# Windowed attention, router and experts: queries and keys turned by DVE in squares of 32, scores of four heads in four row groups

## The chip, the cores and the metric

The program runs on one core of one Trainium2 chip. The metric is the time of one execution on the device in microseconds. The kernel before takes 577.99 us, the median of 3 runs (576.69 to 580.51).

A core has a matrix engine PE (with its weight loads, PEld), a vector engine DVE, a scalar engine ACT, a general engine POOL, and SP, which here only issues transfers. Each runs its own instructions in order; semaphores tie them together.

## The reference

```
scores = (q @ k.T) / sqrt(64)          # q, k, v: batch 4, heads 8, tokens 768, width 64
keep   = key < n_global  or  0 <= query - key < n_local      # 8 and 96 in the given inputs
a      = softmax(where(keep, scores - slope[h] * distance, -1e9))
x      = (a @ v), heads side by side                          # 3072 tokens x 512
logits = normalized(x) @ normalized(expert_emb).T / tau       # 8 experts
e      = argmax(logits);  gate = softmax(logits)[e]
out    = gate * (relu(x @ w1[e]) @ w2[e])                     # w1[e]: 512 x 1024
```

All numbers are float32.

## The kernel before, in words

A group is four heads of one batch, a pair is two of these heads. There are eight groups. Keys come in eight blocks of 96; because the window is at most 97 keys long, a block of keys is scored against its own 96 queries and the next 96. Thirty more key rows per block hold the first tokens of the sequence, the global keys. One block with its 126 key rows is a unit, two units make a step, four steps a group: 32 steps in all, in the loop over `steps` in `window_attention`. The last batch's two groups are interleaved by halves.

`load_tokens` (L367) brings q and k of a pair with token on partition, 128 tokens at a time, in runs of 64 numbers; `load_v` brings v (L373) and its global rows, repeated for each block (L374). SP issues them, two groups ahead. `turn` transposes three tiles of 128x128 with PE (L399) into a PSUM bank, two heads side by side, and ACT copies them to `kT` (L401, L406 for the global rows) and `qT` (L404). `score` (L418) multiplies the 64 rows of each head in one of two row groups of PE: four matmuls a unit, two banks. `grow` takes exp on ACT (L422) and `weigh` multiplies with a table of decay and mask on DVE (L429). `attend` does the step before: output (L444), sums of weights (L452), and after every second step copies out of PSUM: `xd` by ACT (L457) and DVE (L458), `den` by DVE (L463, L465).

When both groups of a batch have finished half of their queries, that half goes through phases, one a step (`half_turns`): PE turns x back to tokens (L516), DVE divides by the sums (L521) and SP stores it, ACT squares it (L526), and the router `choose` works on DVE (L196 to L242), PE, ACT and POOL; POOL then writes the slots with indirect transfers (L245).

The order of every engine's instructions but POOL's is the order in which they are written. Five PSUM banks (`bank`) go round in turn; three more hold the output of `attend`. After attention the first 256 rows of expert 0 are multiplied (L589) while the last slots are written, and then the eight experts run (L968, L904).

Of the kernel before, what the change touches and what calls it, by code (L numbers as in the profile page):

```python
# [32 lines left out]
NB = 8  # L33
# [252 lines left out]
def window_table(k, tmp):  # L286

# [33 lines left out]
    for m in range(2):  # L323
        yield
        for e in range(2):
            for a in range(2):
                nc.scalar.activation(k.table[:, m, e, a], rel[:], AF.Exp, scale=-k.slopes[4 * m + 2 * a + e])
# [3 lines left out]
def window_attention(k, ctx):  # L331

# [4 lines left out]
    def pool(name, bufs, **kw):  # L337
# [6 lines left out]
                 for name, n in (("wa_qk", 4), ("wa_tmp", 1)))  # L344
    kt_p, v_p = pool("wa_kt", 4), pool("wa_v", 3)
    ex_p, late_p, const = pool("wa_ex", 6), pool("wa_late", 2), pool("wa_const", 1)
    xd_p, den_p, xs_p, rt_p = pool("wa_xd", 5), pool("wa_den", 3), pool("wa_xs", 2), pool("wa_rt", 2)
    k.junk = const.tile([P, k.DM], F32, name="junk")
    k.table = const.tile([P, 2, 2, 2, 4, BLK], F32, name="table")
# [6 lines left out]
    def new_pair():  # L356
        t = Net()
        t.k = qk_p.tile([P, NT, 2, D], F32, name="k", tag="k")
        t.q = qk_p.tile([P, NT, 2, D], F32, name="q", tag="q")
        t.qT = kt_p.tile([P, S], F32, name="qT", tag="qT")  # L360
        t.kT = kt_p.tile([P, NB, P], F32, name="kT", tag="kT")
        return t

    def load_tokens(eng, dst, src, b, a, r0, r1):

        for e in range(2):
            eng.dma_start(dst[:, r0:r1, e, :],  # L367
                          src[b, 2 * a + e].rearrange("(t p) d -> p t d", p=P)[:, r0:r1, :])

    def load_v(g, hs):  # L370
        for h in hs:
            src = k.v[g.b, 4 * g.m + h]
            nc.sync.dma_start(g.v[0:BLK, h], src.rearrange("(j r) d -> r j d", r=BLK))  # L373
            nc.sync.dma_start(g.v[BLK:ROWS, h], src[0:GLB].unsqueeze(1).to_broadcast([GLB, NB, D]))  # L374
# [6 lines left out]
    def open_group(g):  # L381
        g.pairs = [new_pair() for _ in range(2)]
        g.v = v_p.tile([P, 4, NB, D], F32, name="v", tag="v")

    def load_part(g, p):
        if p < 2:
            load_tokens(nc.sync, g.pairs[p].k, k.k, g.b, 2 * g.m + p, 0, NT)
            load_tokens(nc.sync, g.pairs[p].q, k.q, g.b, 2 * g.m + p, 0, NT)
        else:
            load_v(g, (2 * p - 4, 2 * p - 3))  # L390
# [3 lines left out]
    def turn(t, i):  # L394

        src, half = (t.k, t.q)[i // 2], i % 2
        ps = bank()
        for r in range(3):
            nc.tensor.transpose(ps[:, r * P : (r + 1) * P], src[:, 3 * half + r, :, :], k.ident[:])  # L399
        if i < 2:  # L400
            nc.scalar.copy(out=t.kT[:, 4 * half : 4 * half + 4, 0:BLK],  # L401
                           in_=ps[:, 0 : 3 * P].rearrange("d (j c) -> d j c", c=BLK))
        else:
            nc.scalar.copy(out=t.qT[:, 3 * half * P : 3 * (half + 1) * P], in_=ps[:, 0 : 3 * P])  # L404
        if i == 0:
            nc.scalar.copy(out=t.kT[:, :, BLK:ROWS], in_=t.kT[:, 0:1, 0:GLB].to_broadcast([P, NB, GLB]))  # L406

    def score(u):

        j, n = u.j, u.n  # L410
        u.sp = [bank() for _ in range(2)]
        u.ex = (late_p if u.late else ex_p).tile([P, 2, 2, 2 * BLK], F32, name="ex", tag="ex")
        u.ex = u.ex[0:ROWS, :, :, 0:n]
        for a in range(2):
            t = u.g.pairs[a]
            for e in range(2):
                rows = slice(e * D, (e + 1) * D)
                nc.tensor.matmul(u.sp[e][0:ROWS, a * n : (a + 1) * n], lhsT=t.kT[rows, j, 0:ROWS],  # L418
                                 rhs=t.qT[rows, j * BLK : j * BLK + n], start=True, stop=True)

    def grow(u, e):
        nc.scalar.activation(u.ex[:, e], u.sp[e][0:ROWS, 0 : 2 * u.n].rearrange("p (a c) -> p a c", a=2), AF.Exp,  # L422
                             scale=k.scale)

    def weigh(u):
        kind = min(u.j, 2)
        tab = k.table[0:ROWS, u.g.m].rearrange("p e a i c -> p (e a) i c")[:, :, kind::(3 - kind), :]
        exv = u.ex.rearrange("p e a (i c) -> p (e a) i c", c=BLK)
        nc.vector.tensor_tensor(out=exv, in0=exv, in1=tab[:, :, 0 : u.n // BLK, :], op=ALU.mult)  # L429

    def attend(g, p):
# [9 lines left out]
        for u, at, c0, c1, first in parts:  # L441
            for a in range(2):
                for e in range(2):
                    nc.tensor.matmul(g.od[a][e * D : (e + 1) * D, at : at + c1 - c0],  # L444
                                     lhsT=g.v[0:ROWS, 2 * a + e, u.j, :],
                                     rhs=u.ex[:, e, a, c0:c1], start=first, stop=True,
                                     skip_group_check=True)
        for u, at, c0, c1, first in parts:
            for a in range(2):
                for e in range(2):  # L450
                    i = 2 * a + e
                    nc.tensor.matmul(g.od[2][32 * i : 32 * i + 32, at : at + c1 - c0], lhsT=k.halves[0:ROWS, g.m].rearrange("p i c -> p (i c)"),  # L452
                                     rhs=u.ex[:, e, a, c0:c1], start=first, stop=True,
                                     skip_group_check=True)
        if p % 2:
            xd = xd_p.tile([P, 2, QB * BLK], F32, name="xd", tag="xd")
            nc.scalar.copy(out=xd[:, 1, :], in_=g.od[1][:, 0 : QB * BLK])  # L457
            nc.vector.tensor_copy(out=xd[:, 0, :], in_=g.od[0][:, 0 : QB * BLK])  # L458
            g.xd.append(xd)
            h, den = p // 2, g.batch.den  # L460
            if g.m == 0:
                den[h] = den_p.tile([P, QB * BLK], F32, name="den", tag="den")
                nc.vector.tensor_copy(out=den[h][:], in_=g.od[2][:, 0 : QB * BLK])  # L463
            else:
                nc.vector.tensor_tensor(out=den[h][:], in0=g.od[2][:, 0 : QB * BLK], in1=den[h][:], op=ALU.add)  # L465
# [78 lines left out]
    def half_turns(hf):  # L544

        t, i = hf.t, 3 * hf.h + hf.phase
        xp = turn_x(t, i) if hf.phase < 3 else None
# [642 lines left out]
```

## Time and profile before

| | |
|---|---|
| median of 3 runs | 577.99 us |
| profiled execution: time, span | 580.19 us, 578.5 us |
| mean granted clock of PE | 0.971 |
| PE busy | 548.2 us (95%) |
| PEld busy | 350.8 us (61%) |
| DVE busy | 164.5 us (28%) |
| ACT busy | 142.3 us (25%) |
| POOL busy | 101.8 us (18%) |
| first scores | 9.63 us |
| last output matmul of attention | ends at 187.45 us |

A share of the whole span is a mean over attention and experts, which have different limits; the stages have to be read one by one. "Busy" is the time in which at least one instruction of an engine runs. The ends of matmuls are modelled, so that matmuls that follow each other overlap on paper; the distance between two starts tells more than a duration. L numbers are lines of the kernel; x and a number count instructions, and PE executes each float32 matmul of the program as two.

### The profile page before, as it was taken

The numbers are of one execution on the slowest core, as the hardware profiler recorded it, in microseconds if no ns is written. First come the engines' busy times: TensorE is split into PE (matmuls) and PEld (weight loads), VectorE is DVE, ScalarE is ACT, GpSimd is POOL, SyncE is SP. The second block draws the span as 40 slices with busy tenths as digits, with TensorE's granted clock in tenths as the row PEclk, the third lists the DMA queues.
The fourth block names the chain that finished last, engine by engine and source line by source line (L and its number), as shares of the span: only waits on it lengthen the run. The fifth ranks groups of instructions, "written<-read, shape, count | busy, mean of one in ns | idle before, by whom it ended". The sixth has DMA issues, their size and how long they took to land.

```text
span 578.5 us, 9188 instructions
## 1 busy us (share of the span) xinstructions
PE 548.2 (95%) x3542; PEld 350.8 (61%) x3542; DVE 164.5 (28%) x411; ACT 142.3 (25%) x336; POOL 101.8 (18%) x130
## 2 busy tenths in 40 slices
PE   8899999999989798999999999999999999999980
PEld 8577788787767676757444447556556444645530
DVE  3254666675775412111000110212101110210010
ACT  4575756756643210001001001001001001001100
POOL 2000015013232225140130013030130130110010
PEclk9799999999989898999999999999999999999995
DMA  8999998994246414543460326443461460010000
GB/s 174 194 186 201 258 254 182 256 235 72 74 128 185 126 25 129 189 150 115 177 238 0 123 84 238 158 142 120 160 232 39 159 226 30 16 43 20 2 36 25
DMA packets 117331, 78.11 MB, mean 135 GB/s; under 512 B 92965, under 2 KB 101157, under 8 KB 117169
## 3 DMA queue, kind: packets, MB, share of 16 engines
q1 hardware_dynamic: 109744, 60.72, 40.9%
q0 software_dynamic: 5536, 15.25, 7.4%
q8 instruction: 51, 0.84, 0.6%
q14 instruction: 112, 0.91, 0.5%
q10 hardware_dynamic: 1888, 0.40, 0.4%
HBM read 63.38 MB, written 13.16 MB: 132 GB/s over the span
## 4 chain that ended last, share of the span: by engine, by line
PE 58%; issue 2%; DMA 1%; POOL 1%; DVE 0%; POOLq 0%
PE big L968 27%; PE work L904 25%; PE work L939 3%; PE work L894 2%; DMA xg<-x_dram,ids 1%; POOL xg L881 0%; POOL out_dram L908 0%; POOL meta L245 0%; DVE y L907 0%; POOLq L1004 0%; DVE flags L1018 0%; POOLq L908 0%; POOLq L881 0%
## 5 line engine op out<-in xcount | busy, mean ns | idle before, releaser
L968 PE MATMUL big<-xT,w1t 128*128 128x320 f32 (+5 forms) x512 | 159.0, 472 | 0.0
L904 PE MATMUL work<-w2t,hT 128*128 128x512 f32 x320 | 139.4, 595 | 0.0
L968 PEld LDWEIGHTS big<-xT,w1t 128*128 128x128 f32 x512 | 95.0, 193 | 64.4 <-issue 31.6
L904 PEld LDWEIGHTS work<-w2t,hT 128*128 128x128 f32 x320 | 60.3, 190 | 74.6 <-issue 73.8
L970 ACT ACTIVATE hT<-big 128x640 f32<-128x640 f32 (+5 forms) x32 | 24.9, 777 | 303.7 <-PE big L968 303.7
L429 DVE TENSOR_TENSOR ex<-ex,table 126x768 f32<-126x768 f32 x64 | 57.7, 904 | 57.9 <-ACT ex L422 55.9
L907 DVE TENSOR_SCALAR y<-work,emt 128x512 f32<-128x512 f32 x22 | 16.5, 751 | 156.7 <-PE work L904 150.0
L422 ACT ACTIVATE ex<-pa 126x384 f32<-126x384 f32 (+1 forms) x128 | 53.3, 476 | 28.8 <-PE pa L418 28.8
L908 POOL DMA_INDIRECT out_dram<-y,ids x22 | 21.8, 992 | 185.6 <-DVE y L907 133.1
L895 DVE COPY xT<-work 128x512 f32<-128x512 f32 x32 | 20.1, 683 | 109.9 <-PE work L894 109.9
L418 PE MATMUL pa<-qT,kT 64*126 64x192 f32 (+1 forms) x512 | 50.7, 336 | 0.4 <-ACT ex L422 0.4
L444 PE MATMUL od<-ex,v 126*64 126x192 f32 (+1 forms) x576 | 48.6, 316 | 0.0
L418 PEld LDWEIGHTS pa<-qT,kT 64*126 64x126 f32 x512 | 41.5, 190 | 10.7 <-issue 6.0
L444 PEld LDWEIGHTS od<-ex,v 126*64 126x64 f32 x576 | 36.0, 142 | 8.8 <-issue 4.7
L881 POOL DMA_INDIRECT xg<-x_dram,ids x34 | 33.3, 981 | 23.0 <-issue 15.6
L245 POOL DMA_INDIRECT meta<-mt,slot x24 | 26.3, 1095 | 38.3 <-DVE good L542 7.8
L452 PE MATMUL od<-ex,halves 126*32 126x192 f32 (+1 forms) x576 | 26.9, 310 | 0.0
L943 POOL DMA_INDIRECT out_dram<-y,pids x7 | 7.1, 1015 | 89.3 <-DVE y L942 84.0
L217 POOL TENSOR_TENSOR ss<-ss,half 128x3 f32<-128x3 f32 (+1 forms) x6 | 6.3, 1047 | 93.0 <-ACT junk L526 93.0
L526 ACT ACTIVATE junk<-xs 128x512 f32<-128x512 f32 x24 | 15.2, 632 | 27.1 <-DVE xs L521 22.2
L939 PE MATMUL work<-w2t,hT 128*32 128x128 f32 (+1 forms) x320 | 20.4, 317 | 0.0
L452 PEld LDWEIGHTS od<-ex,halves 126*32 126x32 f32 x576 | 14.9, 111 | 8.8 <-issue 3.6
(143 smaller groups left out, 389.9 us busy)
## 6 DMA issues: line engine op xcount, KB each, us to landing
w1t<-in_moe_w_dram SPq DMA_DIRECT2D x6, 2048.0 KB, 9.5
w2t<-in_moe_w_dram SPq DMA_DIRECT2D x6, 2048.0 KB, 11.5
v<-in_v_dram SPq DMA_DIRECT2D x32, 192.0 KB, 4.7
x_dram<-xs SPq DMA_DIRECT2D x24, 256.0 KB, 2.8
k<-in_k_dram SPq DMA_DIRECT2D x28, 192.0 KB, 4.0
q<-in_q_dram SPq DMA_DIRECT2D x28, 192.0 KB, 4.2
w1t<-in_moe_w_dram SPq DMA_DIRECT2D x32, 128.0 KB, 3.7
w2t<-in_moe_w_dram SPq DMA_DIRECT2D x32, 128.0 KB, 3.7
```

The source lines that it names most:

```text
L245: i = nc.gpsimd.indirect_dma_start(out=k.meta[:], out_offset=bass.IndirectOffsetOnAxis(ap=slot[:, t : t + 1], axis=0), in_=mt[:, t, :], in ...
L418: nc.tensor.matmul(u.sp[e][0:ROWS, a * n : (a + 1) * n], lhsT=t.kT[rows, j, 0:ROWS], rhs=t.qT[rows, j * BLK : j * BLK + n], start=True, st ...
L422: nc.scalar.activation(u.ex[:, e], u.sp[e][0:ROWS, 0 : 2 * u.n].rearrange("p (a c) -> p a c", a=2), AF.Exp, scale=k.scale)
L429: nc.vector.tensor_tensor(out=exv, in0=exv, in1=tab[:, :, 0 : u.n // BLK, :], op=ALU.mult)
L444: nc.tensor.matmul(g.od[a][e * D : (e + 1) * D, at : at + c1 - c0], lhsT=g.v[0:ROWS, 2 * a + e, u.j, :], rhs=u.ex[:, e, a, c0:c1], start=f ...
L452: nc.tensor.matmul(g.od[2][32 * i : 32 * i + 32, at : at + c1 - c0], lhsT=k.halves[0:ROWS, g.m].rearrange("p i c -> p (i c)"), rhs=u.ex[:, ...
L881: nc.gpsimd.indirect_dma_start(out=xg[:], out_offset=None, in_=k.x_dram[0 : upto or k.N + 1, :], in_offset=bass.IndirectOffsetOnAxis(ap=id ...
L904: nc.tensor.matmul(ps[:], lhsT=hT[:, f, j * P : (j + 1) * P], rhs=w2[:, f, :], start=f == 0, stop=f == k.NF - 1)
L908: nc.gpsimd.indirect_dma_start(out=k.out[:, :], out_offset=bass.IndirectOffsetOnAxis(ap=ids[:, j, 1:2], axis=0), in_=y[:], in_offset=None, ...
L939: nc.tensor.matmul(ps[i * size : (i + 1) * size, 0:m], lhsT=hT[:, f, base : base + size], rhs=w2[:, f, i * m : (i + 1) * m], start=f == 0, ...
L968: nc.tensor.matmul(ps[:, i, 0:w], lhsT=w1[:, c, f * P : (f + 1) * P], rhs=xT[:, c, 0:w], start=c == 0, stop=c == k.NC - 1)
L970: nc.scalar.activation(hT[:, 2 * f2 : 2 * f2 + 2, 0:w], ps[:, :, 0:w], AF.Relu)
```

## The change

q and k of a group's four heads come in one transfer each: partition 32h + i holds the 24 consecutive tokens 24i to 24i + 23 of head h (6,144 bytes in a run). `turn` becomes a DVE transpose in squares of 32x32: each of eight instructions per group turns six tokens of each partition, two squares of 32 numbers per token, and writes to `kT` or `qT`, which hold the four heads in four groups of 32 partitions and the two halves of the width one behind the other. The written elements lie 24 numbers apart. `score` works on both units of a step at once: for each unit and each half y of the width, four matmuls of 32 rows, one a head, in four row groups; the two halves add up in PSUM. One bank and one exp per head and step. `weigh` takes two heads of both units in one instruction where the table rows agree. The DVE's copies of `xd` and of the first `den` go to ACT. v comes in one transfer; its global rows come once, and POOL repeats them for the other seven blocks. At the start the two numbers are asked for first, q and k of the first group come in four pieces each, and all are turned before the first score. In each step the turns come first and both weighings after x has been turned.

```diff
-    def load_tokens(eng, dst, src, b, a, r0, r1):
-        for e in range(2):
-            eng.dma_start(dst[:, r0:r1, e, :],
-                          src[b, 2 * a + e].rearrange("(t p) d -> p t d", p=P)[:, r0:r1, :])
+    def load_tokens(eng, dst, src, g, r0, r1):
+        eng.dma_start(dst[:, r0:r1, :], src[g.b, 4 * g.m : 4 * g.m + 4].rearrange("h (i r) d -> (h i) r d", i=32)[:, r0:r1, :])
+    def load_v(g):
+        nc.sync.dma_start(g.v[0:BLK].rearrange("p h j d -> p (h j) d"),
+                          k.v[g.b, 4 * g.m : 4 * g.m + 4].rearrange("h (j r) d -> r (h j) d", r=BLK))
+    def load_global_v(g):
+        nc.sync.dma_start(g.v[BLK:ROWS, :, 0, :], k.v[g.b, 4 * g.m : 4 * g.m + 4, 0:GLB, :].rearrange("h r d -> r h d"))
+        nc.gpsimd.tensor_copy(out=g.v[BLK:ROWS, :, 1:NB, :],
+                              in_=g.v[BLK:ROWS, :, 0:1, :].to_broadcast([GLB, 4, NB - 1, D]))
...
-    def turn(t, i):
-        src, half = (t.k, t.q)[i // 2], i % 2
-        ps = bank()
-        for r in range(3):
-            nc.tensor.transpose(ps[:, r * P : (r + 1) * P], src[:, 3 * half + r, :, :], k.ident[:])
...
+    def turn(g, what, i):
+        n = S // 32 // 4
+        r = slice(i * n, (i + 1) * n)
+        if what == "k":
+            src, dst = g.k, g.kT[:, :, :, 0:BLK].rearrange("p y b (i r) -> p r y b i", i=4)[:, r]
+        else:
+            src, dst = g.q, g.qT[:].rearrange("p y (i r) -> p r y i", i=32)[:, r]
+        nc.vector.transpose(dst, src[:, r].rearrange("p r (y x) -> p r y x", y=2))
+        if what == "k" and i == 3:
+            for y in range(2):
+                nc.scalar.copy(out=g.kT[:, y, :, BLK:ROWS], in_=g.kT[:, y, 0:1, 0:GLB].to_broadcast([P, NB, GLB]))
+    def score(s, g, us):
+        sp = [bank() for _ in range(4)]
+        ex = ex_p.tile([P, 4, 4 * BLK], F32, name="ex", tag="ex%d" % (...))
+        for i, u in enumerate(us):
+            at = slice(i * 2 * BLK, i * 2 * BLK + u.n)
+            u.ex = ex[0:ROWS, :, at]
+            for y in range(2):
+                for h in range(4):
+                    rows = slice(32 * h, 32 * h + 32)
+                    nc.tensor.matmul(sp[h][0:ROWS, at], lhsT=g.kT[rows, y, u.j, 0:ROWS],
+                                     rhs=g.qT[rows, y, u.j * BLK : u.j * BLK + u.n], start=y == 0, stop=y == 1)
+    def grow(t, h):
+        sp, ex, w = t
+        nc.scalar.activation(ex[:, h, :], sp[h][0:ROWS, 0:w], AF.Exp, scale=k.scale)
+    def weigh(t, us, half):
...
+        if us[0].j and w == 4 * BLK:
+            exv = ex[:, h].rearrange("p h (u c) -> p h u c", u=2)
+            tab = tab[:, :, 2:4].rearrange("p h i c -> p h (i c)").unsqueeze(2).broadcast_to([ROWS, 2, 2, 2 * BLK])
+            nc.vector.tensor_tensor(out=exv, in0=exv, in1=tab, op=ALU.mult)
+        else:
+            for u in us:
...
+                nc.vector.tensor_tensor(out=exv, in0=exv, in1=tab[:, :, kind :: 3 - kind][:, :, 0 : u.n // BLK], op=ALU.mult)
...
-            nc.vector.tensor_copy(out=xd[:, 0, :], in_=g.od[0][:, 0 : QB * BLK])
+            nc.scalar.copy(out=xd[:, 0, :], in_=g.od[0][:, 0 : QB * BLK])
...
-                nc.vector.tensor_copy(out=den[h][:], in_=g.od[2][:, 0 : QB * BLK])
+                nc.scalar.copy(out=den[h][:], in_=g.od[2][:, 0 : QB * BLK])
...
+    next(numbers)
     build_consts(k)
...
+    for i in range(4):
+        load_tokens(nc.sync, first.k, k.k, first, 6 * i, 6 * i + 6)
+        load_tokens(nc.scalar, first.q, k.q, first, 6 * i, 6 * i + 6)
+    load_v(first)
+    for h in range(4):
+        nc.scalar.dma_start(first.v[BLK:ROWS, h], k.v[0, h, 0:GLB].unsqueeze(1).to_broadcast([GLB, NB, D]))
...
-    busy(8)
+    busy(24)
...
+    for i in range(4):
+        turn(first, "k", i)
+        turn(first, "q", i)
...
+        pieces = [(g, x, i) for x in "kq" for i in range(4)]
         at = [4 * gi - 4 + i // 2 for i in range(8)]
...
+        if gi == 1:
+            at = [1, 1, 2, 2, 2, 3, 3, 3]
         elif gi == len(groups) - 1:
+            at = [4 * gi - 4 + i // 4 for i in range(8)]
...
+        for x in turns[s]:
+            turn(*x)
+        now = score(s, g, us)
...
+        for hf in active:
+            turn_half(hf)
+        weigh(now, us, 0)
+        weigh(now, us, 1)
+        for hf in active:
+            route_half(hf)
```

`turn_half` and `route_half` are the two parts of `half_turns`: the sums, the turn of x and its store; and the products, the router's next stage and the check of the sums. The buffers of `ex` are named by step (four in turn, another order in the last eight steps), and the buffers of q, k, `qT` and `kT` hold two groups, as before.

## The prediction

> **What bounds the kernel now.** The first view is the table of stages: busy time of each engine in chosen stretches. Its columns are the stretch and its length, then busy microseconds and instructions of PE, weight loads (PEld), DVE, ACT and POOL, then the granted clock, the DMA share and GB/s.
>
> ```profile
> core 0: us, PE busy (x) PEld busy (x) DVE busy (x) ACT busy (x) POOL busy (x), PEclk, DMA share, GB/s
> 0.00:36.15 36.15, 31.46 (x257) 25.32 (x257) 13.45 (x36) 19.89 (x49) 5.62 (x31) 0.91 1.10 183
> ...
> 96.70:138.37 41.67, 41.67 (x534) 33.35 (x531) 27.41 (x58) 27.05 (x71) 8.34 (x8) 1.00 0.99 218
> ...
> 187.45:225.55 38.10, 31.99 (x143) 23.64 (x139) 11.82 (x50) 6.32 (x15) 11.71 (x12) 0.89 0.34 92
> 225.55:578.50 352.95, 336.91 (x1282) 184.96 (x1282) 41.92 (x107) 24.86 (x32) 54.82 (x56) 0.98 0.32 113
> ```
>
> Attention (32 steps) ends at 187.45 us. The routing tail and the experts after it hold nothing that the change edits, so they move with the end of attention. The second row is one whole batch, eight steps: PE has no idle time in 41.67 us, DVE and ACT are busy for 27 each. From 36.15 to 151.29, 115.14 us or 2.76 such batches, PE sets the pace. The time line of PE in one step shows on what:
>
> ```profile
> 101.52 1.57 PE L418 MATMUL pa<-qT,kT 64*126 64x192 f32 x16
> 103.02 0.55 PE L399 MATMUL pa<-ident,q 128*128 128x128 f32 x3
> 103.41 0.49 PE L399 MATMUL pa<-ident,k 128*128 128x128 f32 x3
> 103.73 0.60 PE L516 MATMUL pa<-ident,xd 128*128 128x128 f32 x4
> 104.26 1.52 PE L444 MATMUL od<-ex,v 126*64 126x192 f32 x16
> 105.72 0.86 PE L452 MATMUL od<-ex,halves 126*32 126x192 f32 x16
> ```
>
> Scores, two turns (q and k), a turn of x, attention output, sums. The opening is different; there PE waits for data:
>
> ```profile
> 18.33 0.52 PE L399 MATMUL pa<-ident,k 128*128 128x128 f32 x3 [1.54 <-DMA k<-in_k_dram]
> 20.12 1.30 PE L399 MATMUL pa<-ident,q 128*128 128x128 f32 x5 [1.27 <-DMA q<-in_q_dram]
> ```
>
> **PE's part.** Six transposes take 103.73 - 103.02 = 0.71 us where a turn of x follows in the same shape of array; elsewhere (37.64 to 38.45) 0.81 with the change of shape. I take 0.75 a step, 6.0 a batch: PE falls from 41.7 to 35.7. The scores become 16 matmuls of 32 rows for 8 of 64 rows. The trace shows the 8 as 16 records, in two row groups at a time; the 1.57 above is 8 rounds of some 0.16 and a tail. L452's 16 records run in four column groups at a time: 0.86 for 4 rounds. If four row groups do the same, the new 32 records are again 8 rounds: no cost. The other end, two at a time, costs 8 x 0.16 = 1.3 us a step. I take none, by L452, the nearest row with four groups.
>
> **DVE's part** decides. From its 27.4 a batch go four copies L458 and two L463:
>
> ```profile
> L429 DVE TENSOR_TENSOR ex<-ex,table 126x768 f32<-126x768 f32 x56 | 53.4, 954 | 57.9 <-ACT ex L422 55.9 <-ACT table L327 1.8
> L458 DVE COPY xd<-od 128x384 f32<-128x384 f32 x16 | 8.8, 550 | 4.2 <-PE od L444 4.2
> L508 DVE TENSOR_REDUCE lg<-lh 128x24 f32<-128x192 f32 x8 | 4.0, 505 | 0.3
> L196 DVE TENSOR_REDUCE m<-lg 128x3 f32<-128x24 f32 x4 | 0.7, 170 | 0.0
> ```
>
> That is 6 x 0.55 = 3.3. The weighing keeps two instructions of 768 elements in half of the steps. Step 0 of a group takes four of 384 (0.55 each) for two of 768: +0.3. Step 3 takes two of 384 and two of 192 (about 0.35) for one of 768 and one of 384: +0.3. With two groups, +1.2. So 25.3 a batch without the turns, and 16 turns come on.
>
> No row shows a DVE transpose. Each moves 384 elements, reads densely and writes single elements 96 bytes apart. From below: a dense pass of 384 is 0.55 us (L458). L508 reads elements 32 bytes apart: 505 ns for 192, where the fixed part is about 146 (170 for L196's 24, 198 for 48 elements), hence 1.87 ns an element against 1.04 dense. With that for the writes: 0.146 + 384 x 1.87 = 0.87 us. From above: if reading and spaced writing do not overlap, 0.146 + 384 x (1.04 + 1.87) = 1.27. I take 0.87, because L508 is the only large strided access in the trace. DVE instructions start some 0.08 before the one in front ends, so a turn occupies 0.79 (0.47 dense, 1.19 at the upper end). 25.3 + 16 x 0.79 = 37.9.
>
> [...]
>
> POOL's new copy (30 rows x 1,792 elements, two a batch) is the second unknown. POOL's copies take 178 ns for 6 elements and 208 for 32, about 1 ns each, so 2.0 us; by its slowest rows (TENSOR_SCALAR 249 ns for 6 and 362 for 48) 5. What it does to DVE is seen here from the other side:
>
> ```profile
> 149.47 0.95 DVE L429 TENSOR_TENSOR ex<-ex,table 126x768 f32<-126x768 f32 x1
> 149.87 0.60 POOL L243 COPY mt<-tok 128x6 f32<-128x6 f32 x1
> ```
>
> A POOL copy that takes 0.18 elsewhere ended only when the weighing ended. If a long POOL copy holds the weighing alike, DVE loses between 0 and 5 us each; I take half of 2.0, so 2.2 a batch. [...]
>
> DVE: 37.9 + 2.2 = 40.1, more than PE's 35.7. DVE becomes the bound, and PE waits for weighed scores. I add 0.6 for the step in which PE cannot take its fourth score bank before DVE has read the router's counts (154.25, PE waits 0.55 for L221 now): **40.7**. Gain (41.67 - 40.7) x 2.76 = 2.7.
>
> **Costed at nothing.** ACT loses eight kT and eight qT copies a batch (7.9 us) and gets six (2.8): about 22 of 41, far from bound. Its four exps now start together after the last score, but they start 0.38 apart and PE has 2.2 us of attend in between; without that cover, 1.3 us a step. New waits: POOL's copy waits for the transfer of its rows, and behind it in POOL's order stand only the router's power (L217) and the slot writes, which the end of attention needs in the last batch alone, when all copies are done. On DVE the weighing now stands behind x (L521), which waits for PE's turn of x; that turn comes right after the scores, before the exps are done, so it adds nothing. SP issues fewer transfers than now. The larger transfers of q and k bring nothing after 36 us: no PE wait for them is in the list there.
>
> **The opening.** Tables need the two numbers, whose transfer is now issued first (about 1.2 instead of 4.6; read 3.1 later, at 4.3). Then 0.8 + 3.2 us of DVE as now gives 8.3, and eight turns 6.3: first scores at 14.6 (now 9.63). Until the third bank of step 1 is free: 1.5 + 0.2 + 3 exps at 0.38 + four table exps at 0.44 = 4.6, so 19.2. Scores and attend 3.9: 23.1. Then two steps with three turns each on DVE, 2.4 + 1.8: 27.3 and 31.5, against 36.15: -4.7. Step 1's 12.4 us, with late data and a clock of 0.69, go.
>
> **The last group's turns** fall into steps 24 and 25, four each. Step 25 now takes 7.24 with DVE busy for 5.83; 5.83 - 0.55 + 4 x 0.79 = 8.4: +1.2. Step 24: 2.54 + 3.2 = 5.7 against 5.68: none. Step 26 loses its PE turns: -0.75. Together +0.5.
>
> **Sum for the profiled execution** (span 578.5, time 580.19): -2.7 - 4.7 + 0.5 = -6.9, so 573.3. It was 2.2 slower than the median 577.99, so the median becomes **571**. About 1% (572.2 to 583.8) is what a measurement here tells from no change. This case itself runs from 563 to 583 with what POOL's copy holds.
>
> **Rivals.**
> PE stays the bound: a turn is dense, 0.47. DVE 25.3 + 7.5 + 2.2 = 35.0; PE 35.7 + 1.5 for the heavy routing steps: 37.2, gain 12.4; opening 12.1 first scores, -7.3; tail -2. In all -21.7: **556**. L458 speaks for it, L508 against.
> Slower: DVE is overrun by the turns alone. At 1.19: 25.3 + 19.0 + 2.8 = 47.1, +15.0; opening +1.4; tail +3.8: +20, 598. A tenth of a microsecond per turn costs 4.4 + 1.4 + 0.8 = 6.6, so -6.9 turns to a loss from an occupied 0.90, a duration of about 1.0 us, only 0.13 above my figure. Its middle, 1.13, gives **588**. 64 turns and L508 speak for it.
> The row groups don't do what they say: two at a time. PE 35.7 + 10.4 + 0.6 = 46.7, +13.9; opening and tail +4: **596**. L452 speaks against it.
>
> **Numbers.** Chances: DVE-bound forecast 0.38, PE-bound 0.28, overrun 0.24, row groups 0.10. Range 557 to 592: it takes in most of the PE-bound case and most of the overrun. Faster by over 1%: 0.28 + 0.16 = 0.44; slower: 0.23 + 0.10 + 0.02 = 0.35; the rest 0.21.
>
> **What would show it.** One transpose row on DVE with its mean; DVE busy above 95% of a batch and PE waiting for ex before L444; score records four at a time, about 0.16 apart; weighings longer than 0.96 next to the POOL copy; first scores near 14.6. A mean near 0.55 or above 1.0, or rounds of 0.3, makes the prediction wrong.

## The result, and the profile after

The changed kernel is slower: median 596.73 us (593.33 to 600.35), the kernel before 579.07 us beside it. The ratio is 1.031, 95% interval 1.0231 to 1.0389. The profiled execution took 598.54 us, its span is 596.7 us: 18.2 more than before. All ratios are of fast runs; the profiled execution of e1_dense was a slow one (601.56 us, the other three 592.46 to 597.08), so no time of a step or of the whole is taken from its trace.

The starts of single steps show where the time goes (steps count from 0 to 31, profiled executions, us). The last column is what the prediction expected of each stretch; its 2.7 us for the batches are put down by length to the stretches before and after step 24.

| stretch | before | after | difference | predicted |
|---|---|---|---|---|
| start to step 4 | 36.15 | 37.51 | +1.4 | -4.7 |
| step 4 to 24 | 102.22 | 110.02 | +7.8 | -2.4 |
| step 24 to 31 | 41.07 | 47.58 | +6.5 | +0.2 |
| step 31 to the end | 399.06 | 401.59 | +2.5 | 0 |

The table of stages of the changed kernel has the same columns as the one of the kernel before: stretch, busy time and instructions of PE, PEld, DVE, ACT and POOL, granted clock, DMA share, GB/s.

```profile
core 0: us, PE busy (x) PEld busy (x) DVE busy (x) ACT busy (x) POOL busy (x), PEclk, DMA share, GB/s
0.00:37.51 37.51, 29.79 (x293) 25.02 (x293) 26.65 (x54) 13.86 (x35) 7.32 (x30) 1.00 1.06 213
...
58.44:104.88 46.44, 42.20 (x614) 31.93 (x611) 38.40 (x76) 22.80 (x61) 9.95 (x9) 0.89 0.72 183
104.88:147.53 42.65, 38.09 (x615) 29.41 (x611) 37.16 (x75) 22.68 (x61) 11.78 (x10) 1.00 0.70 187
...
161.16:203.10 41.94, 35.79 (x507) 27.09 (x504) 24.16 (x73) 19.03 (x52) 12.01 (x15) 0.88 0.43 127
```

Two rows are whole batches. PE, which had no idle time in the batch of 41.67 us before, now is idle for 4.2 and 4.6 us of a longer batch. DVE is busy for 38.4 and 37.2, idle for 8.0 and 5.5. So neither engine is the bound. In two of the stretches the granted clock fell to 0.89 and 0.88. The 1.00 of the opening is not a measured value: this trace has no record of the clock before 28.8 us, and up to there rounds of scores start 0.32 us apart, where they later start 0.16 apart.

The groups of DVE instructions, by form, give the prices that the prediction had to guess (the last columns: busy, mean ns | idle before):

```profile
L401 DVE STREAM_TRANSPOSE qT<-q 128x384 f32<-128x384 f32 x32 | 33.3, 1139 | 0.0
L432 DVE TENSOR_TENSOR ex<-ex,table 126x768 f32<-126x768 f32 x32 | 31.4, 1021 | 11.4 <-ACT ex L423 11.4
...
L401 DVE STREAM_TRANSPOSE kT<-k 128x384 f32<-128x384 f32 x32 | 24.2, 825 | 0.0
```

A turn of k takes 0.83 us, one of q 1.14. The next instruction starts 0.68 us after a turn of k and 0.93 after one of q, on average 0.81; the prediction had 0.79. The list of waits names what PE waits for instead (us in total, times, longest):

```profile
PE pa L491 <- DVE den L473: 12.5, 5, 3.6
```

L491 turns the sums of weights of a half, the denominators of the softmax. Before the change PE waited nowhere between 55 and 138 us. The time line shows one of the five waits and what follows it. In the last line the same instruction group stands as it looks in an undisturbed step.

```profile
93.35 2.08 DVE L401 STREAM_TRANSPOSE qT<-q 128x384 f32<-128x384 f32 x2
93.40 1.34 PE L416 MATMUL pa<-qT,kT 32*126 32x192 f32 x32
...
95.22 1.85 DVE L432 TENSOR_TENSOR ex<-ex,table 126x768 f32<-126x768 f32 x2
...
97.00 0.55 DVE L473 TENSOR_TENSOR den<-od,den 128x384 f32<-128x384 f32 x1
...
97.69 0.87 PE L491 MATMUL pa<-ident,den 128*128 128x128 f32 x3 [2.95 <-DVE den L473]
...
99.34 3.47 PE L452 MATMUL od<-ex,v 126*64 126x96 f32 x24
...
121.81 1.85 PE L452 MATMUL od<-ex,v 126*64 126x96 f32 x24
```

PE has written the sums at 93.4 and multiplied the next scores by 94.7. The sum `den` on DVE (L473) stands behind two turns and two weighings, comes at 97.00, and PE idles for 2.95 us. Then it runs at half pace, with a granted clock of 0.50 from 97.07 to 103.90: the output that takes 1.85 elsewhere takes 3.47. This step, number 15, lasts 11.48 us; before the change it lasted 6.21. In the kernel before, the same turn of the sums (there L483) came without a wait:

```profile
89.86 0.70 PE L452 MATMUL od<-ex,halves 126*32 126x192 f32 x16
90.49 1.33 PE L418 MATMUL pa<-qT,kT 64*126 64x192 f32 x16
91.75 0.55 PE L399 MATMUL pa<-ident,q 128*128 128x128 f32 x3
92.13 0.49 PE L399 MATMUL pa<-ident,k 128*128 128x128 f32 x3
92.46 0.60 PE L516 MATMUL pa<-ident,xd 128*128 128x128 f32 x4
92.89 0.49 PE L483 MATMUL pa<-ident,den 128*128 128x128 f32 x3
```

Between the last matmul of the sums and their turn PE had 2.3 us of scores and turns. Now it has 1.3 us of scores alone.

### The profile page after: what moved, and what is told of

Its sections match the earlier page's. It is cut to its first block, busy times and chain, and to the rows that moved or that the text cites. A ratio compares the mean times of both kernels' runs of the same rounds, so it can differ in the third digit from the quotient of the medians.

```text
span 596.7 us, 9796 instructions
## 1 busy us (share of the span) xinstructions
PE 545.4 (91%) x3882; PEld 345.4 (58%) x3882; DVE 210.5 (35%) x483; ACT 125.1 (21%) x296; POOL 113.4 (19%) x137
## 4 chain that ended last, share of the span: by engine, by line
PE 65%; DVE 4%; DMA 2%; ACT 1%; issue 1%; POOL 1%; POOLq 0%; DVEq 0%; ACTq 0%
PE big L965 27%; PE work L901 25%; PE work L936 3%; PE work L891 2%; PE pa L598 2%; PE od L452 2%; PE pa L416 1%; DMA x_dram<-xs 1%; PE od L460 1%; DMA xg<-x_dram,ids 1%; DVE ex L437 1%; ACT ex L423 1%; DVE ex L432 1%; PE pa L213 1%; DVE xs L529 1%
## 5 line engine op out<-in xcount | busy, mean ns | idle before, releaser
L416 PE MATMUL pa<-qT,kT 32*126 32x192 f32 (+1 forms) x1024 | 58.5, 342 | 6.8 <-DVE ok L123 4.6
L416 PEld LDWEIGHTS pa<-qT,kT 32*126 32x126 f32 x1024 | 47.8, 193 | 19.0 <-issue 4.8
L423 ACT ACTIVATE ex<-pa 126x384 f32<-126x384 f32 (+1 forms) x128 | 49.9, 476 | 28.0 <-PE pa L416 27.8
L452 PE MATMUL od<-ex,v 126*64 126x192 f32 (+1 forms) x576 | 53.4, 337 | 1.0 <-ACT xd L466 1.0
L452 PEld LDWEIGHTS od<-ex,v 126*64 126x64 f32 x576 | 39.0, 153 | 11.9 <-issue 4.8
L432 DVE TENSOR_TENSOR ex<-ex,table 126x768 f32<-126x768 f32 x32 | 31.4, 1021 | 11.4 <-ACT ex L423 11.4
L437 DVE TENSOR_TENSOR ex<-ex,table 126x384 f32<-126x384 f32 x64 | 32.4, 565 | 7.0 <-ACT table L325 4.6
L401 DVE STREAM_TRANSPOSE qT<-q 128x384 f32<-128x384 f32 x32 | 33.3, 1139 | 0.0
L366 POOL COPY v<-v 30x1792 f32<-30x1792 f32 x7 | 12.3, 1753 | 88.2 <-DMA v<-in_v_dram 73.0
L401 DVE STREAM_TRANSPOSE kT<-k 128x384 f32<-128x384 f32 x32 | 24.2, 825 | 0.0
```

Source lines behind the costliest of these rows:

```text
L401: nc.vector.transpose(dst, src[:, r].rearrange("p r (y x) -> p r y x", y=2))
L416: nc.tensor.matmul(sp[h][0:ROWS, at], lhsT=g.kT[rows, y, u.j, 0:ROWS], rhs=g.qT[rows, y, u.j * BLK : u.j * BLK + u.n], start=y == 0, stop= ...
L423: nc.scalar.activation(ex[:, h, :], sp[h][0:ROWS, 0:w], AF.Exp, scale=k.scale)
L432: nc.vector.tensor_tensor(out=exv, in0=exv, in1=tab, op=ALU.mult)
L437: nc.vector.tensor_tensor(out=exv, in0=exv, in1=tab[:, :, kind :: 3 - kind][:, :, 0 : u.n // BLK], op=ALU.mult)
```

## The experiments

All edits are made to the changed kernel unless said. Ratios are to the kernel before on the same chip; on two of the five chips of these experiments, that kernel itself took 587 us instead of 579 to 580, so ratios and starts of steps are compared, not times across chips.

| run | edit | median us (before beside it) | ratio, 95% |
|---|---|---|---|
| (changed kernel) | | 596.73 (579.07) | 1.031, 1.023 to 1.039 |
| e1_dense | dense turns, runs of 256 bytes | 596.88 (579.28) | 1.026, 1.018 to 1.033 |
| e2_sums_late | sums behind attention output | 593.03 (579.28) | 1.020, 1.013 to 1.027 |
| e3_no_pool_copy | no copy by POOL | 590.97 (579.28) | 1.017, 1.010 to 1.024 |
| e4_copies_later | global keys behind exps | 592.53 (579.28) | 1.020, 1.014 to 1.027 |
| e5_runs3 | runs of 768 bytes | 591.27 (579.90) | 1.018, 1.010 to 1.026 |
| e6_den_ahead | attention output ahead of weighings | 590.95 (579.90) | 1.019, 1.016 to 1.023 |
| e7_fill | PE fed during a wait | 600.02 (579.90) | 1.035, 1.028 to 1.041 |
| e8_three | e2, e3 and e4 | 585.85 (579.90) | 1.011, 1.007 to 1.016 |
| e9_put_back | PE's old work put back | 612.04 (586.86) | 1.046, 1.042 to 1.050 |
| e10_three_runs3 | e8 and e5 | 596.85 (586.86) | 1.020, 1.015 to 1.025 |
| e11_pieces | e10, first turns in pieces | 592.60 (586.86) | 1.011, 1.007 to 1.015 |
| e12_pieces_den | e11 and e6 | 591.56 (586.86) | 1.010, 1.006 to 1.013 |
| e13_dense_only | dense turns, transfers unchanged | 587.12, one run (579.57) | |
| e14_three_dense | e8 and e13 | 574.55, one run (579.57) | |
| e15_three_again | e8 again | 585.98 (579.57) | 1.011, 1.008 to 1.015 |
| e16_four | e8 and e6 | 590.30 (579.57) | 1.018, 1.013 to 1.022 |
| e17_order_qdense | e8, dense q, PE reads it with a step | 615.56 (587.25) | 1.049, 1.045 to 1.052 |
| e18_order_qdense_xs4 | e17, four buffers for x | 612.78 (587.25) | 1.042, 1.038 to 1.046 |

### Cheaper turns with other transfers

Theory A was that DVE is overloaded by the turns; theory B that the order of instructions makes the waits. The first edit leaves out the wide spacing of a turn's writes. Partition i then holds the tokens 32r + i, which come in runs of 256 bytes:

```diff
-    src[g.b, 4 * g.m : 4 * g.m + 4].rearrange("h (i r) d -> (h i) r d", i=32)
+    src[g.b, 4 * g.m + h].rearrange("(r i) d -> i r d", i=32)      # for each head
-    dst = g.qT[:].rearrange("p y (i r) -> p r y i", i=32)[:, r]
+    dst = g.qT[:].rearrange("p y (r i) -> p r y i", i=32)[:, r]    # kT alike
```

> Edit: partition 32h + i holds the tokens 32r + i (runs of 64 numbers, one transfer a head, as many as before the change), so that a DVE turn writes 32 numbers one behind the other; all else as in the changed kernel. Theory A (DVE is overloaded in single steps, and the turns' price decides): a turn occupies 0.47 like the dense copy instead of 0.72 (k) and 0.89 (q). With the dearer of PE and DVE taken in each of the eight steps of a batch I get 41.6 us with the turns as they are (the trace: 42.65 at full clock) and 38.7 with these; times 2.76 batches -8, the slow clock in steps 8 to 16 gone -5, opening -2.6: about 580. Theory B (the waits come from the order of instructions, sums ahead of x and weighings behind x, whatever the turns cost): 592 or more. If spaced writes are not what a turn pays for, its mean stays at 0.83 and 1.14 and the time at 597.

```profile
L405 DVE STREAM_TRANSPOSE kT<-k 128x384 f32<-128x384 f32 x32 | 16.5, 551 | 9.9 <-DMA k<-in_k_dram 9.9
L405 DVE STREAM_TRANSPOSE qT<-q 128x384 f32<-128x384 f32 x32 | 16.5, 550 | 4.5 <-DMA q<-in_q_dram 4.5
```

These are the same groups in this run. Turns fell to 0.55 us, the price of a dense copy (L458 before, 0.55), so spaced writes are what the others pay for; and the time stayed. But the last column is new: DVE waits 14 us for k and q, and it waits 16.6 for the stores of x. The DMA engines were busy 1.25 of the time between 36 and 59 us, against 0.61 between 37.5 and 58.4 in the changed kernel. The gain may have gone there, so this run does not decide. The next edit takes runs of three tokens (768 bytes), writes 12 bytes apart:

> Edit: partition 32h + i holds, of each block of 96 tokens, the three tokens 3i to 3i + 2 (runs of 768 bytes, one transfer a head), so that a turn writes single numbers 12 bytes apart. The run with tokens 32r + i had turns of 0.55 but waited for its transfers of 256-byte runs (DVE idle 14 us in front of turns, 17 in front of x for its stores). Theory A (DVE is overloaded in single steps), now without that: a turn of 0.55 to 0.70, no wait of DVE for k or q, batches of 39.5 to 41, opening -2: 580 to 585. Theory B' (PE's waits are a chain of latencies, scores, four exps, two weighings, den, sums, which DVE's load hardly lengthens): 592 or more, with the step of phase 0 still at 8 to 11 us.

A turn takes 0.68 us, both of k and of q; DVE waits 5.8 us for k and q. The ratio is 1.018 with an interval of 1.010 to 1.026, which overlaps that of the changed kernel (1.023 to 1.039). The wait for `den` did not go: 2.2 us in step 15, with the slow output behind it (3.45 us for 1.85), and that step lasted 9.4. As far as this goes B is favoured, with transfers still mixed in (DMA share 1.12 between 36 and 100 us, 0.70 before the edit).

### One wait at a time

```diff
-        for hf in active:
-            turn_half(hf)
+        for hf in active:
+            if hf.phase:
+                turn_half(hf)
 ...    # and behind attend(q, qp)
         for hf in active:
             if hf.phase == 0:
+                turn_half(hf)
                 score_experts(hf, bank())
```

> Edit: in phase 0 of a half (steps 7 and 2 of eight) the turn of the sums and of x stands behind the attention output of the step, not in front of it, and on DVE the reciprocal and x behind both weighings. Theory B (order): PE's waits for den, 1.0 and 3.3 us a batch in steps 16 to 24, 2.5 in step 29, fall behind 2.2 us of attention output; about -3 a batch, and the slow clock that follows them goes too (-5): about 584. Theory A (DVE is behind by its load): the wait moves to the attention output, which needs weighings that stand just in front of den on DVE, and to the next phase; 592 or more.

Step 15 fell from 11.48 to 7.97, step 29 from 11.70 to 7.62; ratio 1.020. Between the two expectations: in phase 0 PE now waits 1.4 and 0.3 us for weighings (L432) in the attention output instead of 3 for `den`. The longest of them in step 15:

```profile
95.97 0.55 PE L452 MATMUL od<-ex,v 126*64 126x192 f32 x4 [1.41 <-DVE ex L432]
```

The next edit moves ACT's copies of the global keys.

```diff
-        if what == "k" and i == 3:
-            for y in range(2):
-                nc.scalar.copy(out=g.kT[:, y, :, BLK:ROWS], ...)
 ...    # in the step, behind grow(now, 3)
+        for g2, what, i in turns[s]:
+            if what == "k" and i == 3:
+                globals_of(g2)         # the same two copies
```

> Edit: ACT's two copies of the global keys stand behind the four exps of the step, not in front of them, where they wait for the step's turns on DVE. If that order costs what the trace shows at 112.96 (exps start 2.1 us after the scores, PE waits 1.0 in the next scores), the time falls by 1.0 in each of six groups and 2 in the opening or less: 590 to 593. If DVE's load decides, the next instruction of DVE is late anyway: 596 to 597.

This one starts from three lines of the changed kernel's time line:

```profile
112.37 0.69 ACT L404 COPY kT<-kT 128x240 f32<-128x240 f32 x2 [2.76 <-DVE kT L401]
...
112.96 1.62 ACT L423 ACTIVATE ex<-pa 126x384 f32<-126x384 f32 x4
...
113.59 2.60 PE L416 MATMUL pa<-qT,kT 32*126 32x192 f32 x32
```

The scores of that step were ready at 110.8. ACT's copies wait for a turn on DVE, the exps stand behind them, and the next scores, which need the banks that the exps empty, take 2.60 instead of 1.58. With the copies behind the exps those scores follow without the wait (step 18 lasts 5.13 instead of 5.87). Right here this gains nothing, since in the step before PE now waits 0.6 us for the router's products (L515), and that step lasts 5.02 instead of 4.34; the clearest gain is step 6, 3.27 instead of 4.96. The ratio is 1.020, the size expected. Part of it is the clock, which stayed at 1.00 in step 7 (6.32 us instead of 8.95).

```diff
-        nc.gpsimd.tensor_copy(out=g.v[BLK:ROWS, :, 1:NB, :], in_=g.v[BLK:ROWS, :, 0:1, :].to_broadcast(...))
+        for h in range(4):
+            nc.sync.dma_start(g.v[BLK:ROWS, h], k.v[..., 0:GLB].unsqueeze(1).to_broadcast([GLB, NB, D]))
```

> Edit: the global rows of v come for all eight blocks by one transfer a head, as before the change; POOL copies nothing. Theory C (the lock of POOL's copy on the weighings): four or five weighings were longer by 0.7 to 1.5 us next to the seven copies, in all some 6 us of DVE; -6 if each lies on the path: 591. Theory A or B: these hits fall where DVE has idle time in the same batch, and the opening keeps 1.5 of it: 595. All weighings of 768 elements at 0.95 then, in every theory.

All weighings of 768 elements then take 0.955 on average. In the changed kernel (time line of the opening; two weighings take 1.83 elsewhere):

```profile
25.34 3.31 DVE L432 TENSOR_TENSOR ex<-ex,table 126x768 f32<-126x768 f32 x2 [0.44 <-ACT ex L423]
...
26.06 1.77 POOL L366 COPY v<-v 30x1792 f32<-30x1792 f32 x1 [21.17 <-DMA v<-in_v_dram]
```

Six of seven copies lengthened a weighing, by 0.5 to 1.5 us, 6.4 in all. The ratio of 1.017 is the size that theory C gave.

The last of these edits writes `attend(*steps[s - 1])` ahead of `weigh(now, us, 0)`, so that `den` stands in front of the weighings:

> Edit: the attention output of the step before is written ahead of the step's weighings and routing; on DVE the sum den so stands in front of the two weighings of its step, on PE the attention output in front of the routing's matmuls. Theory B' (chain of latencies through den and oh): PE's waits for den (2 to 3 us, in steps 7, 15, 23, 29) and for oh (1.4 to 1.8, once a batch) go, with the slow clock behind them: 583 to 588. Theory A (DVE's load in these steps): PE waits as long for the weighings, which now stand behind den: 594 or more.

Ratio 1.019: alone it helps (steps 15 and 23 last 7.40 us each, with 1.6 us of wait for `den` left in either), though a new wait came too: 3.5 us for a bank that holds the router's products (L514).

Each of these single ratios is below that of the changed kernel by 0.011 to 0.014, with intervals that touch or overlap; one by one they do not prove much.

### What a wait costs: the clock

```diff
         ps = bank()
+        if h == 0:
+            for _ in range(10):
+                nc.tensor.matmul(ps[:, 0:64], lhsT=k.ones[:], rhs=k.ones[:, 0:64], start=True, stop=True)
```

> Edit: in front of the turn of the sums of each first half PE multiplies ten times 64 columns into the bank that the sums will overwrite (about 2.2 us of PE at full clock), so that PE is not idle while it waits for den. Theory D (what the waits cost is in good part PE's clock, which falls to 0.5 for some 5 us after an idle time of 3): steps 15 and 23 fall from 9.0 to 11.7 to 8.5, 29 too; -6 to -8 in all: 589 to 591. If the clock doesn't matter or falls anyway: 597 to 601.

```profile
96.83 1.28 PE L492 MATMUL pa<-ones 128*128 128x64 f32 x10
...
98.59 0.55 PE L494 MATMUL pa<-ident,den 128*128 128x128 f32 x3 [0.48 <-DVE den L473]
...
99.51 1.85 PE L452 MATMUL od<-ex,v 126*64 126x96 f32 x24
```

That is step 15 with PE fed through the wait. The output takes 1.85, not 3.47; the step lasts 8.49 us, not 11.48, and its granted clock is 1.00, not 0.70. So of the 11.48 some 3 us were the clock. The changed kernel shows the same without an edit. Its step 23 has a longer wait for `den`, 3.30 us, and keeps its clock; the first row is step 15, the second step 23:

```profile
93.40:104.88 11.48, 8.53 (x99) 6.06 (x96) 9.74 (x17) 2.78 (x8) 5.91 (x6) 0.70 0.47 89
138.50:147.53 9.03, 5.73 (x100) 4.28 (x96) 8.87 (x18) 3.25 (x10) 6.33 (x6) 1.00 0.35 63
```

The wait alone makes step 23 2.8 us longer than before the change (6.21); in step 15 the clock about doubles that. The length of the wait alone does not tell whether the clock falls; what else decides was not tried. The whole run gained nothing (1.035): the filling costs PE time in every first half, and steps 27 and 12 were longer, 9.24 and 8.73 for 6.45 and 7.90; why is open.

### PE's old work put back

```diff
         sp = [bank() for _ in range(4)]
+        if 0 < s < 27:
+            for i in range(6):
+                nc.tensor.transpose(sp[0][:, i % 3 * P : i % 3 * P + P], k.ident[:], k.ident[:])
```

> Edit: the changed kernel with PE's old work put back: in steps 1 to 26 PE turns the unit matrix six times (0.7 us) into the first score bank, in front of the scores. If PE's time sets the step, as it did before the change: 26 x 0.71 = +18, about 615. Theory B' (a chain through ACT and DVE sets the steps, and PE's own turns had lain beside it): PE has 4 to 6 us of waits a batch and slow clock besides, so it costs +0 to +6: 597 to 603.

```profile
93.78 0.87 PE L411 MATMUL pa<-ident 128*128 128x128 f32 x6
94.59 1.34 PE L419 MATMUL pa<-qT,kT 32*126 32x192 f32 x32
```

26 times 0.8 us of PE work, 21 in all, raised the ratio by 0.015, some 9 us (the intervals leave 4 to 14), and the start of the last step by 7.5 us, between the two expectations and nearer to the second. About half of the PE work that the change saves, or more, had therefore bought nothing: put back, it fell into time in which PE waited anyway.

### The waits together, and the turns apart

> Edit: three earlier edits at once: the sums of phase 0 behind the attention output, ACT's copies of the global keys behind the exps, the global rows of v by transfers instead of POOL's copy. Alone they gave 593.0, 592.5 and 591.0 against 596.7. If they take different waits away they add up to -15: 582. If all three only let DVE catch up in the same steps: 590.

> The three edits of order once more, on this chip: 585.9 there, ratio 1.011; the same here, 1.007 to 1.016.

Sums behind the attention output, copies behind the exps and no copy by POOL take the ratio from 1.031 to 1.011 on two chips, and the intervals no longer meet. The last step starts at 181.5 and 180.5 instead of 195.1. Still open was what the turns cost when nothing else moves. The next kernel writes dense turns from the transfers of the changed kernel, so that tokens lie at other positions; x and the routing are then other numbers, and only the steps of attention are compared.

> Edit: the changed kernel with turns that write 32 numbers one behind the other, with the transfers as they are. This mixes the positions of the tokens in q and k, so x and the routing are not the reference's, and only the times up to the end of the attention steps are compared. DVE loses 16 x 0.33 = 5.3 us a batch. If DVE's load sets the steps: steps 8 to 24 in 80 instead of 89 us, start of step 24 near 135 instead of 147.5. If the chain of waits does: steps 8 to 24 in 85 or more, start of step 24 at 142 or later.

> Edit: the same dense turns (positions mixed, only the attention steps compared) and the three edits of order (sums behind the attention output, copies of the global keys behind the exps, global rows by transfers). With the three edits alone steps 8 to 24 took 80.5 us and the last step began at 181.5. If then DVE's load is the next bound: steps 8 to 24 in 74 (PE's 36 a batch and 1 of waits), start of the last step near 170. If not: 79 and 179.

| start of step (us) | 4 | 8 | 24 | 31 | steps 8 to 24 |
|---|---|---|---|---|---|
| before | 36.15 | 55.02 | 138.37 | 179.44 | 83.35 |
| after | 37.51 | 58.44 | 147.53 | 195.11 | 89.09 |
| dense turns alone (e13) | 39.34 | 56.47 | 138.12 | 185.32 | 81.65 |
| three waits alone (e15) | 37.99 | 53.99 | 134.48 | 180.46 | 80.49 |
| both (e14) | 32.27 | 48.93 | 126.37 | 167.50 | 77.44 |

The table of stages for steps 8 to 24, first dense turns alone, then the three edits, then both:

```profile
56.47:138.12 81.65, 77.10 (x1224) 58.87 (x1221) 67.37 (x154) 45.51 (x122) 22.18 (x19) 0.96 0.81 204
```

```profile
53.99:134.48 80.49, 77.61 (x1225) 58.20 (x1221) 74.30 (x151) 45.52 (x122) 16.08 (x16) 1.00 0.85 221
```

```profile
48.93:126.37 77.44, 76.26 (x1224) 56.75 (x1220) 63.35 (x154) 45.32 (x122) 15.68 (x15) 1.00 0.99 239
```

Each lever shortens these two batches by 7 to 9 us, both by 11.7, to 38.7 a batch; PE is then idle for 1.2 us in 77. At the start of the last step they give 9.8 and 14.7 alone and 27.6 together, 11.9 ahead of the kernel before. So both theories were half right. The three waits (two by order, one by POOL's copy) and the spaced writes each cost about as much as the change could bring, and the clock multiplied the waits: with the three gone it is 1.00 in these steps. In e13 step 3 took 12.0 us, since PE waited 5.0 for the expert vectors; the 9.8 is a low figure for that reason. e13 and e14 are one execution each, and executions of the changed kernel lie up to 7 us apart (593.33 to 600.35), so these gains are sizes and not exact figures.

> Edit: the three edits of order and the attention output ahead of weighings and routing, with the transfers of the changed kernel. PE's waits for oh (5.1 us in the three edits' run) should go and nothing else be late: -3 to -5, ratio 1.002 to 1.007. If the weighings are late instead, as the run with all edits and 768-byte runs showed (4.9 us of PE's waits for ex): 1.010 to 1.015.

On top of the three edits, `den` ahead of the weighings is a loss: 1.018 against 1.011 on the same chip. PE's waits for weighings rose from 2.0 to 4.3 us, and steps with a finished half grew (step 9: 5.24 for 4.33). What helped while `den` was late hurts when it no longer is.

### Towards a faster kernel

> Edit: the three edits of the run that gave 585.9 (sums behind the attention output, copies of the global keys behind the exps, no copy by POOL) and turns that write 12 bytes apart (0.68 instead of 0.83 and 1.14). If DVE is the bound once the waits by order are gone (in that run DVE stood 4.0 us in four turns of the last group, and x behind them): -5 to -8: 578 to 581. If DVE's load does not matter: 584 to 586.

> Edit: the last one and, beside it, the first group's turns only as far as the first scores need them (one of k, two of q, the rest while ACT makes the table), its transfers in two pieces, and the other groups' turns put into steps with less work on DVE, the last group's over three steps instead of two. The opening should give first scores at 12 instead of 17.5 and step 4 at 34 instead of 39 (-5), the tail -2 to -3: 571 to 575, below the kernel before. If the opening is bound by late data or exps: 577 to 580.

> Edit: the last one with the attention output of the step before written ahead of the weighings and the routing. If PE's waits for oh and den are what is left in the batches, another -2 to -4 against the run without it; if the weighings then stand in the way (they come up to 1.5 later in two steps of eight), +0 to +3.

The first two missed, and the third differs from the second by less than the noise (1.010 and 1.011). With the smaller transfers DVE waits 16.6 us for stores of x in the first of them. The pieces brought first scores at 11.55 instead of 15.2, and step 4 at 35.0; then k and q of the next group came late (DVE waits 12.8 us for both). 768-byte runs thus give back what cheaper turns win; that it is the DMA engines' load is the reading that fits the waits, and no run changed that load alone.

The right result with dense q and the large transfers needs PE to read q with a step of 32 numbers:

```diff
-    rhs=g.qT[rows, y, u.j * BLK : u.j * BLK + u.n]
+    rhs=g.qT[rows, y, :].rearrange("p (r i) -> p i r", i=32)[:, 4 * u.j : 4 * u.j + u.n // 24, :]
```

> Edit: the three edits of order (585.98, ratio 1.0112, last step at 180.5), and q's turns write 32 numbers one behind the other; the scores read q with a step of 32 numbers, so the tokens are in order; k's turns, transfers and result as in the changed kernel. q's turns are two thirds of what dense turns save. If PE reads as fast with the step: two thirds of 13 us, so last step at 172, 577 us, ratio 0.994 to 1.000. If the step costs PE time in the scores (rounds of more than 0.16): each 0.05 a round is 0.4 us a step, 13 in all, and the gain is gone: 1.01.

> Edit: the last one, and four buffers for the turned x instead of two. DVE's waits for the stores of x (3.5 us with the three edits, 11.4 with both levers) go. If they lay on the path: -2 to -4 against the run without; if beside it: 0.

```profile
112.81 2.87 PE L416 MATMUL pa<-qT,kT 32*126 32x192 f32 x32
```

The scores of a step take 2.87 instead of 1.58, and the ratio is 1.049. More buffers for x bring back 0.007, with intervals that just touch. None of the kernels with the reference's result beats the kernel before; the nearest are at 1.010 and 1.011.

## Why the prediction was wrong, by its own steps

- **PE's part** held in steps without routing: step 22 lasts 3.27 us in e14 and 4.06 before, 0.79 for the 0.75 taken. A whole batch came out smaller: with nearly all waits gone (e14) PE is busy for 38.1 and the batch takes 38.7, where the sum was 35.7, or 37.2 with the steps of routing in the first rival.
- **The four row groups** held. The scores of a step are 32 records in 1.58 us, where 16 took 1.57; four start together, every 0.16 us. The rival that they do not is out.
- **A turn's price** held on average where it counts: 0.81 occupied for 0.79. In duration it is 0.83 and 1.14, mean 0.98, for 0.87. That a price measured on a read with a step (L508) was near a write with a step is luck in part: q pays more and k less. Dense turns took 0.55 (e1_dense), as the dense copy L458 does, on which the first rival stood.
- **POOL's copy** held: 6.4 us on weighings where half of 2.0 for each of seven copies was taken. (The span "563 to 583" does not follow from 0 to 5 us a copy; with two copies a batch the same sum gives 565 to 593.) The one turn beside such a copy was not touched: it took 1.16 from 48.50 on, the copy ran from 48.59 to 50.26, and turns of q take 1.10 to 1.17 anyway. Why the copy holds weighings and not this turn was not tried.
- **The sum for DVE** held within 3 us: 37.9 and 2.2 for POOL's hold, 40.1 in all, against 38.4 and 37.2 measured. **The step that failed comes next: "DVE becomes the bound", 40.7 a batch.** A batch took 46.4 and 42.65 with DVE idle for 5 to 8 of it, busy for 83 and 87% and not above 95, and PE waited for `den` and not for weighed scores. (Once three waits are gone, e15, a batch takes 40.2; the sum without POOL's hold is 38.5.) The period was taken as the busy sum of the fullest engine plus 0.6, as if work could be shifted within a batch. The engines here run in order (in step 17 exps whose scores were ready stood 2.1 us behind copies that waited) and are tied to each other once or twice a step.
- What hides these ties is the subject of **"Costed at nothing"**, and that is where the 0.6 was too small. Three waits together measured 13.6 and 14.7 us at the start of the last step (e8, e15), POOL's hold included, for which the sum had 2.2 a batch. The place of ACT's copies of the global keys was not looked at: they stand in front of the exps and hold them by 2.6 us in step 5, 2.1 in steps 9 and 17, 1.7 and 0.7 in steps 24 and 21, and hardly in the other two. The turn of the sums was moved ahead of the turn of x and lost the six turns that used to stand between the sums' last matmul and it: in first halves 1.3 to 1.4 us of cover are left of 2.3, and all four waited, 1.7 to 3.6 us. The second halves of the first two batches have 2.4 and 2.5 us of cover, 2.6 before, and did not wait. The weighings behind x wait with x: in five places DVE waits, 14.2 us in all, in front of x for PE; what this alone costs was not tried.
- **The clock** was in no term. Step 15 loses 3 us to it (e7); of the stretches, those at 0.88 and 0.89 lost most. Between steps 4 and 31 the mean granted clock is 0.92 in 157.6 us, and it was 0.99 in 143.3 before; worked out from these, an estimate, the clock took up to some 11 of the 14.3 us lost there (less what PE was idle in the slow stretches).
- **The opening** was forecast at 31.5 for step 4 and came at 37.5. The numbers were read at 5.54, not 4.3; the eight turns took 6.5 for 6.3; first scores at 16.23, not 14.6. Step 1 came another 1.3 later than that shift explains, with scores and attention output at half pace: from the first scores to 28.8 PE's rounds lay 0.32 us apart, while before the change they lay 0.16 apart at 14.3 (granted clock 1.00), and the clock was 0.50 from 19.4 to 26.2; step 2 another 3.0 later, 1.5 of it POOL's copy on a weighing. Dense turns and the three edits together bring 32.3.
- **The last group's turns** were to cost 0.5; steps 24 to 31 lost 6.5. Steps 24 and 25 took 0.7 more, near the +1.2. The rest is waits and clock in steps 26, 27 and 29 (clock 0.88).
- From step 31 on 2.5 us are lost with the same work; 2.15 of them lie in the experts, where PE is busy for 2.1 more. That stays open.

Of the rivals, "overrun" named the right sign and more of the size (588), but by luck: its price is a duration of 1.13, and the mean is 0.98 (q alone has 1.14). With order and writes both mended the PE-bound rival appears (37.2 a batch there, 38.7 in e14), though not its time: e14's one execution took 574.55, the rival 556.

## What to carry to other kernels

Where engines run in order and meet in every step, the busy sum of a long stretch is a lower bound and not a forecast: follow one step's chain (scores, exps, weighings, sum, next step's turn) with the cover that is left once the removed work is gone. Work that is taken off the bounding engine can have been cover for others, so look first at what it hid. Before giving a move of data to another engine, look at how it writes: here the spacing cost about as much as the move saved, the step on the reader's side cost more (1.049 for 1.011), and the smaller runs on the transfer's side brought nothing once the waits were gone (1.020 for 1.011).

## What the runs showed of the hardware that was not expected

- A DVE turn of 128x384 float32 in squares of 32 takes 0.55 us with dense writes, 0.68 with writes 12 bytes apart, 1.14 with 96 bytes (q) and 0.83 for k, whose writes are 96 bytes apart in fours and then jump to another block. Why k is cheaper than q was not tried.
- PE reading its moving operand with a step of 128 bytes needs some 0.32 us for each round of four row groups (2.87 us for the eight rounds of a step's scores in e17), where it needs 0.16 (1.58 us) without one.
- In the changed kernel idle times of 1.72, 2.95 and 3.63 us in front of the sums were followed by a granted clock of 0.50 for 3.4, 6.8 and 6.8 us, and one of 3.30 by none. In e5_runs3 the output behind an idle time of 2.17 us took 3.45 us for 1.85, and where PE was fed through the gap the clock stayed at 1.00 (steps 15 and 23 of e7_fill).
